# Modulation sums interleaved with the first norm, and the second row block loaded from ScalarE's queue

## The chip, the core and the metric

The kernel runs on one core of one Trainium2 chip. The metric is the device time of one launch in microseconds. The core's engines run side by side, each taking its own instructions in the order in which they were built: TensorE (PE, with its weight loads as PEld), VectorE (DVE), ScalarE (ACT), GpSimd (POOL) and SyncE (SP). SP and ACT also start transfers (DMAs): such a start is an instruction in that engine's own stream, shown in the trace as SPq or ACTq.

## The reference

One block with adaptive layer norm, in float32, on 2048 rows of 512 columns:

```python
mod = (_silu(c) @ w_mod).reshape(c.shape[0], 6, 1, -1)
sa, ca, ga, sb, cb, gb = (mod[:, 0], ..., mod[:, 5])
h = _layernorm(x, axis=-1) * (1 + ca) + sa
x = x + ga * _A_ref(h, A_dft_seq_re, A_dft_seq_im, A_dft_hid_re, A_dft_hid_im)
h = _layernorm(x, axis=-1) * (1 + cb) + sb
x = x + gb * _B_ref(h, B_w1, B_w3, B_w2)
```

`_A_ref` multiplies by a 512 x 512 transform along the columns and a 2048 x 2048 transform along the rows and keeps the real part; `_B_ref` is a gated product through 1792 hidden columns. Only the very first part matters here: the norm of the first rows, the two modulation vectors `sa` and `1 + ca` (six vectors come from one matrix of 512 x 3072; these two are needed first), and the first products along the columns.

## The kernel before

The rows are handled in eight row blocks k of 2 x 128 rows (a block of rows and its mirror image, the two "sides"). Each block is loaded, normed, turned with TensorE, modulated, added to and subtracted from its mirror image, split into a high and a low part, and multiplied with the weights of the column transform. Those weights come in four blocks (`load_hid`, tile `w`), each of four loads of 64 x 512; ScalarE copies a high part (`w_highs`, tile `wu`), VectorE takes the low part (`w_lows`) and ScalarE a negated copy (`w_minus`, tile `wn`).

The modulation vectors are sums over 512 rows of `w_mod`. `v` is 1 for `1 + ca` and 0 for `sa`; each comes as two tiles `wmr` (h = 0, 1) with two groups of 128 rows in each (n = 0, 1). ScalarE scales the first group by `silu(c)` (L335), VectorE adds the three others onto it (L307), four matmuls against ones then sum over the partitions into a bank (`mod_sum`, L314), and VectorE reads the bank into `mod` (`mod_read`, L324). Only then can ScalarE modulate the turned rows (`hm`, L501).

What comes before the modulated rows of block 0 is written out by hand in the order shown in the diff below. Everything behind that is put in order by a planner (`arrange`) with a table of ranks and estimated times of its own; its table is not touched. `keep_warm` issues matmuls whose result is not used. `clear_z` copies zeros into a tile that the first bank of products is begun with (`hid_begin`, L549). In the norm, `norm_stats` is L449 and L450, `norm_root` a square root on ScalarE (L454), `norm_inverse` L459 and L460, `norm_scale` L468 and L470, and `turn_rows` L485.

Loads are tracked by eight semaphores, taken in turn (DMAHW0 to DMAHW7 below). A load that takes a semaphore which an earlier load used is held, on the engine that starts it, until that earlier load has landed.

```python
    nc.sync.dma_start(cc, cp)
    load_x(0, nc.scalar)
    load_wm(1, 0, nc.scalar)
    load_wm(1, 1, nc.sync)
    load_wm(0, 0, nc.scalar)
    load_wm(0, 1, nc.sync)
    for dt in range(2):
        load_hid(dt, nc.sync)
    load_x(1)
```

Of the kernel before, what the change touches and what calls it, by code (L numbers as in the profile page):

```python
# [12 lines left out]
OP = mybir.AluOpType  # L13
AX = mybir.AxisListType

P = 128
# [26 lines left out]
def folded(nc, pools, c, cp, wmr, wmc, x, xt, ctr, cti, wdr, wdi, w1, w3, w2, out):  # L43
# [15 lines left out]
    def take(dt=F32, what="s"):  # L59
        slot = free.popleft()  # L60
        count[0] += 1
        t = big.tile([P, 2, N], dt, name=f"{what}_{count[0]}", tag=f"slot{slot}")
        slot_of[id(t)] = (slot, t)
        return t

    def give(t):
        slot, _ = slot_of.pop(id(t))
        free.append(slot)

    def bank(i):  # L70
        count[0] += 1
        return psum.tile([P, N], F32, name=f"bank{i}_{count[0]}", tag=f"bank{i}")

    def flat(t):
        return t.rearrange("p a b -> p (a b)")
# [7 lines left out]
    def cols(i):  # L83
        return slice(i * P, (i + 1) * P)

    def copy(dst, src, scale=1.0):
        nc.scalar.activation(dst, src, AF.Copy, scale=scale)  # L87
# [57 lines left out]
    def where(k):  # L145
        return k % (NK // 2), 1 - k // (NK // 2)
# [19 lines left out]
    def load_mirror(dst, src, k, t=None):  # L166
        i, par = where(k)
        rows = src.rearrange("i p q n -> (i p q) n" if t is None else "t i p q n -> (t i p q) n")
        at = mirror[:, t or 0, 1 - par, i : i + 1]
        nc.gpsimd.indirect_dma_start(  # L170
            dst, None, rows, bass.IndirectOffsetOnAxis(ap=at, axis=0)
        )
# [25 lines left out]
    xz = {}  # L198

    held = consts.tile([1, 1], F32, name="held")  # L200

    def load_x(k, other=nc.sync):
        if k >= NK // 2:
            nc.gpsimd.tensor_copy(held, wd[0][0:1, 1, 0:1].bitcast(F32))


        i, par = where(k)
        xz[k] = take(F32, "x")
        nc.sync.dma_start(xz[k][:, 0, :], x[i][par::2])
        if par:  # L210
            other.dma_start(xz[k][:, 1, :], x[NK - 1 - i][1::2])
        else:
            load_mirror(xz[k][:, 1, :], x, k)

    wm = {}
# [10 lines left out]
    def load_hid(dt, queue):  # L226
        i, par = HD[dt]
        raw_w[dt] = take(F32, "w")
        for m, w in enumerate((wdr, wdi)):
            for q in range(2):  # L230
                queue.dma_start(raw_w[dt][q * 64 : (q + 1) * 64, m, :], w[i][par::2, q])
# [6 lines left out]
    load_wm(0, 1, nc.sync)  # L238
    for dt in range(2):
        load_hid(dt, nc.sync)  # L240
    load_x(1)
    for dt in range(2, ND):
        load_hid(dt, nc.sync)
    for k in range(2, 4):
# [26 lines left out]
    zero = take(F32, "zero")  # L271
    nc.gpsimd.memset(flat(zero), 0.0)
    first_tmp = take(F32, "tmp")
    onesf = first_tmp[:, 0, :]
# [3 lines left out]
    def keep_warm(count, width=N):  # L278

        for _ in range(count):  # L280
            nc.tensor.matmul(
                warm[:, :width], onesf[:, :P], onesf[:, :width], start=True, stop=True
            )

    sc = consts.tile([P, ND], F32, name="sc")
# [8 lines left out]
    def hid_cols(t, dt):  # L294

        i, par = HD[dt]
        return t[:, 2 * P * i + par : 2 * P * (i + 1) : 2]

    mod_acc = [bank(5), bank(6)]

    def mod_scale(v, h):

        w, own = wm[v, 0][:, 0, :], wm[v, h]
        if h == 0:
            copy_by(w, w, sc[:, 0:1])
        for n in range(1 - h, 2):
            nc.vector.scalar_tensor_tensor(  # L307
                w, own[:, n, :], sc[:, 2 * h + n : 2 * h + n + 1], w, op0=OP.mult, op1=OP.add
            )

    def mod_sum(v):

        for dt in range(ND):
            nc.tensor.matmul(  # L314
                mod_acc[v][:, cols(dt)],
                hid_cols(wm[v, 0][:, 0, :], dt),
                onesf[:, :P],
                start=True,
                stop=True,
            )  # L320

    def mod_read(v):
        for at in (slice(0, ND),) if v else [slice(dt, dt + 1) for dt in range(ND)]:
            nc.vector.tensor_scalar(  # L324
                mod1[:, v, at],
                mod_acc[v][:, ::P][:, at],
                float(v),
                None,
                op0=OP.add,
            )  # L330
        for h in range(2):
            give(wm.pop((v, h)))

    def copy_by(dst, src, by):
        nc.scalar.activation(dst, src, AF.Identity, scale=by)  # L335
# [106 lines left out]
    def norm_stats(k, side):  # L442
        if side == 0:
            rs[k] = (
                small.tile([P, 2, 2], F32, name=f"mv_{k}", tag="mv"),
                small.tile([P, 2, 2], F32, name=f"rs_{k}", tag="rs"),
            )
        st = small.tile([P, 6], F32, name=f"st_{k}_{side}", tag="st")
        nc.vector.bn_stats(st, xz[k][:, side, :])  # L449
        nc.vector.bn_aggr(rs[k][0][:, side, :], st)  # L450

    def norm_root(k):
        mv, r = rs[k]
        nc.scalar.activation(r[:, 0, :], mv[:, :, 1], AF.Sqrt, bias=eps, scale=1.0)  # L454

    def norm_inverse(k):

        mv, r = rs[k]
        nc.vector.reciprocal(r[:, 0, :], r[:, 0, :])  # L459
        nc.vector.scalar_tensor_tensor(  # L460
            r[:, 1, :], mv[:, :, 0], -1.0, r[:, 0, :], op0=OP.mult, op1=OP.mult
        )
# [17 lines left out]
    def turn_rows(k, side):  # L480
        if side == 0:
            turned[k] = [bank(2 * (k % 2) + h) for h in range(2)]
        for dt in range(ND):
            at = (dt % 2) * HALF + side * P
            nc.tensor.transpose(  # L485
                turned[k][dt // 2][:, at : at + P],
                hid_cols(xz[k][:, side, :], dt),
                anti if side and where(k)[1] else ident,
            )
        if side:  # L490
            give(xz.pop(k))
            rs.pop(k)
# [48 lines left out]
    nought = consts.tile([P, P], F32R, name="nought")  # L541
# [4 lines left out]
    def hid_begin(k):  # L546

        hb[k] = bank(4 + k % 2)
        nc.tensor.matmul(  # L549
            hb[k], nought, flat(wt[0] if k else zz)[:, :N], start=True, stop=False, skip_group_check=True  # L550
        )
# [102 lines left out]
    def clear_z():  # L654
        copy(flat(zz), flat(zero))
        give(zero)
# [838 lines left out]
    }  # L1495
    seq_steps = []
    keep_warm(3)
    for side in range(2):
        norm_stats(0, side)
    norm_root(0)  # L1500
    norm_inverse(0)
    for side in range(2):
        norm_scale(0, side, "ACT" if side else "DVE")
        turn_rows(0, side)
    keep_warm(1)
    for v, h in ((1, 0), (1, 1), (0, 0)):
        mod_scale(v, h)
    mod_sum(1)
    copy(nought, zero[:, 0, :P])
    clear_z()  # L1510
    hid_begin(0)
    keep_warm(6, P)
    mod_scale(0, 1)
    mod_read(1)
    mod_sum(0)
    mod_read(0)


    at(10.0, "turn0.0", "turn0.1")
# [18 lines left out]
    for k in range(NK):  # L1538
        r = k * PACE
        both = [f"{k}.0", f"{k}.1"]  # L1540
        if k:
# [10 lines left out]
            for s in range(2):  # L1552
                task(
                    f"scale{k}.{s}", r + RANK["scale"] + s, [f"inverse{k}"],
                    lambda e, k=k, s=s: norm_scale(k, s, e), ACT=0.71, DVE=0.46,
# [5 lines left out]
        for dt in range(ND):  # L1561
            task(
                f"mod{k}.{dt}", r + RANK["mod"] + 0.1 * dt, [f"modc{dt}", *[f"turn{n}" for n in both]],
                lambda e, k=k, dt=dt: modulate_rows(k, dt, e), ACT=0.45, DVE=0.46,
# [1068 lines left out]
```

## Time and profile before

| | us |
|---|---|
| three runs | 691.91, 692.39, 694.4 |
| median of them | 692.39 |
| the profiled execution | 690.63 |
| its span, first to last instruction | 688.8 |
| first matmul on modulated rows (L559) begins | 21.82 |
| TensorE busy in the span | 672.4 (98%) |

The span lies 1.83 us under the profiled execution's own time, and that execution 1.76 us under the median. Times in the views are us from the span's start, and a duration follows a start. The granted TensorE clock is 0.997 over the span.

### The profile page before, as it was taken

To read this page: it belongs to the slowest core of one execution; us is meant where nothing else is said; L and a number is where in the kernel's file an instruction comes from. 1 tells how busy PE (TensorE), PEld (TensorE's weight loads), DVE (VectorE), ACT (ScalarE), POOL (GpSimd) and SP (SyncE) were. 2 spreads that over 40 slices of the span, in tenths; PEclk is the share of its full clock that TensorE was granted. 3 is DMA by queue.
4 is the path that set the end of the run, shared out by engine and by line. 5 is a ranking of instruction groups with operands and counts; after the bars stand their busy time and mean duration, and the time that the engine had idled before them with its cause. 6 is when DMAs were issued, how large, how long until landed. Compare 5 with 4: busy or idle time off the path is not lost.

```text
span 688.8 us, 9035 instructions
## 1 busy us (share of the span) xinstructions
PE 672.4 (98%) x3122; PEld 557.4 (81%) x3122; DVE 586.8 (85%) x945; ACT 451.2 (65%) x751; POOL 132.2 (19%) x156
## 2 busy tenths in 40 slices
PE   6999999999999999999999999999999999999996
PEld 4898788888888888888788888887887888888785
DVE  5999769998999987989997989787998979888465
ACT  4998956455343665663577767867687887877620
POOL 1320162543435000100101001011011112221100
PEclk9999999999999999999999999999999999999998
DMA  8740299787679440274767666475859998999713
GB/s 264 224 124 1 54 368 339 249 297 258 197 287 291 154 151 30 46 139 122 119 141 141 150 153 121 94 128 118 267 108 183 175 203 167 181 214 173 179 45 127
DMA packets 40837, 116.80 MB, mean 170 GB/s; under 512 B 5200, under 2 KB 5456, under 8 KB 40784
## 3 DMA queue, kind: packets, MB, share of 16 engines
q0 software_dynamic: 14512, 50.86, 36.9%
q1 hardware_dynamic: 25840, 63.98, 28.1%
q10 hardware_dynamic: 432, 1.31, 0.6%
q8 instruction: 26, 0.43, 0.3%
q14 instruction: 27, 0.22, 0.1%
HBM read 76.81 MB, written 41.42 MB: 172 GB/s over the span
## 4 chain that ended last, share of the span: by engine, by line
PE 84%; DVE 9%; ACT 4%; issue 1%; DMA 1%; SPq 0%; DVEq 0%; ACTq 0%
PE bank L100 54%; PE bank L750 26%; PE bank L559 2%; PE bank L598 1%; ACT hm L501 1%; DMA x<-in_x 1%; DVE xr L806 1%; DVE st L449 1%; PE bank L576 1%; DVE v L96 1%; DVE hl L90 0%; DVE ul L90 0%; DVE x L93 0%; ACT hh L87 0%; DVE w3s L90 0%
## 5 line engine op out<-in xcount | busy, mean ns | idle before, releaser
L100 PE MATMUL bank<-hf,w2h 128*128 128x512 f32 (+1 forms) x352 | 108.3, 389 | 0.0
L87 ACT ACTIVATE hf<-v 128x512 fp32r<-128x512 f32 x71 | 44.4, 631 | 66.7 <-DVE v L96 53.9
L335 ACT ACTIVATE y<-bank,gb 128x512 f32<-128x512 f32 x118 | 76.5, 682 | 3.9 <-PE bank L100 3.6
L100 PEld LDWEIGHTS bank<-hf,w2h 128*128 128x128 f32 x352 | 65.6, 188 | 15.4 <-ACT y L335 1.5
L1161 POOL DMA_DIRECT2D sum<-y x28 | 24.0, 857 | 240.7 <-ACT y L335 124.5
L100 PE MATMUL bank<-hf,w2l 128*128 128x512 f32 (+1 forms) x176 | 68.1, 387 | 0.0
L90 DVE TENSOR_TENSOR hf<-v,hf 128x512 fp32r<-128x512 f32 x71 | 48.7, 685 | 10.6 <-ACT hf L87 10.5
L1353 POOL DMA_DIRECT2D sum<-y x35 | 29.8, 852 | 128.3 <-ACT y L335 120.8
L87 ACT ACTIVATE x<-bank 128x512 f32<-128x512 f32 x72 | 41.7, 591 | 13.6 <-PE bank L100 12.7
L750 PE MATMUL bank<-d,uh 128*128 128x512 f32 x128 | 49.9, 390 | 0.0
L750 PE MATMUL bank<-l,us 128*128 128x512 f32 x128 | 49.9, 390 | 0.0
L750 PE MATMUL bank<-d,us 128*128 128x512 f32 x128 | 49.9, 390 | 0.0
L750 PE MATMUL bank<-bh,us 128*128 128x512 f32 x128 | 49.9, 390 | 0.0
L750 PE MATMUL bank<-bh,ul 128*128 128x512 f32 x128 | 49.8, 389 | 0.0
L750 PE MATMUL bank<-l,uh 128*128 128x512 f32 x128 | 49.8, 389 | 0.0
L170 POOL DMA_INDIRECT re<-in_ctr,mirror x32 | 35.7, 1115 | 66.6 <-ACT im L188 40.1
L170 POOL DMA_INDIRECT im<-in_cti,mirror x32 | 32.9, 1028 | 33.4 <-DVE l L90 8.9
L100 PEld LDWEIGHTS bank<-hf,w2l 128*128 128x128 f32 x176 | 33.1, 188 | 6.6
L93 DVE TENSOR_TENSOR v<-bank,x 128x512 f32<-128x512 f32 x36 | 24.7, 686 | 15.6 <-PE bank L100 14.0
L1245 ACT ACTIVATE v<-v 128x512 f32<-128x512 f32 x36 | 22.6, 629 | 22.7 <-DVE v L93 22.4
L93 DVE TENSOR_TENSOR x<-bank,x 128x512 f32<-128x512 f32 x36 | 24.7, 685 | 14.5 <-PE bank L100 13.7
L188 ACT ACTIVATE im<-l 128x512 f32<-128x512 f32 x16 | 10.1, 632 | 32.4 <-DVE d L93 15.5
(260 smaller groups left out, 1922.4 us busy)
## 6 DMA issues: line engine op xcount, KB each, us to landing
sum<-y POOLq DMA_DIRECT2D x63, 512.0 KB, 5.7
w<-in_w SPq DMA_DIRECT2D x42, 512.0 KB, 4.8
re<-in_ctr SPq DMA_DIRECT2D x32, 256.0 KB, 5.8
im<-in_cti SPq DMA_DIRECT2D x32, 256.0 KB, 5.3
wmc<-in_wmc SPq DMA_DIRECT2D x8, 512.0 KB, 7.2
sum<-xr SPq DMA_DIRECT2D x8, 512.0 KB, 5.6
x<-in_x SPq DMA_DIRECT2D x11, 256.0 KB, 4.5
xr<-in_xt SPq DMA_DIRECT2D x8, 256.0 KB, 7.1
```

The lines of the kernel that those rows point to most:

```text
L87: nc.scalar.activation(dst, src, AF.Copy, scale=scale)
L90: nc.vector.tensor_tensor(out=dst, in0=a, in1=b, op=OP.subtract)
L93: nc.vector.tensor_tensor(out=dst, in0=a, in1=b, op=OP.add)
L100: nc.tensor.matmul(acc, lhs[a], rhs[b], start=first and n == 0, stop=last and n == len(PASSES) - 1, skip_group_check=more,)
L170: nc.gpsimd.indirect_dma_start(dst, None, rows, bass.IndirectOffsetOnAxis(ap=at, axis=0))
L188: nc.scalar.activation(to, src.bitcast(F32), AF.Square, accum_out=chk[:, kind, KINDS.index(m), n : n + 1],)
L335: nc.scalar.activation(dst, src, AF.Identity, scale=by)
L559: nc.tensor.matmul(halves(hb[k])[:, m, :], sides((hh, hl)[a][k])[:, dt, m, :], wu[dt][:, b, m, :], start=False, stop=dt % 2 == 1 and n == ...
L750: nc.tensor.matmul(acc[what, e], lhs, rhs, start=begin and i == 0, stop=(end or (turn and what == "x")) and i == len(terms) - 1, skip_grou ...
L1161: nc.gpsimd.dma_start(sums[t, d // 2], y, accum_op=OP.add)
L1245: behind(k != 0 or q == 0, lambda: nc.scalar.activation(v, src, AF.Silu))
L1353: nc.gpsimd.dma_start(sums[t, which], y, accum_op=OP.add)
```

## The change

The zeros are copied right at the start. The first scaling and the first addition for `v = 1` stand ahead of and behind the square root of the norm. The first matmul that was only there to keep TensorE busy becomes one that writes zeros over the whole bank for `v = 0`; that vector's sum over the partitions is then made in two parts, one for tile h = 1 (whose first group ScalarE scales, where VectorE added it before) and one for tile h = 0 with the rest added onto it. The load of row block 1 leaves SP's queue, where it stood between the second and the third block of column weights, and is issued from ScalarE's instruction stream behind its modulation copies.

```diff
-    def load_x(k, other=nc.sync):
+    def load_x(k, other=nc.sync, one=nc.sync):
...
-        nc.sync.dma_start(xz[k][:, 0, :], x[i][par::2])
+        one.dma_start(xz[k][:, 0, :], x[i][par::2])
...
-    load_x(1)
     for dt in range(2, ND):
         load_hid(dt, nc.sync)
...
-    def mod_scale(v, h):
-
+    def mod_copy(v, h, n):
+        w = wm[v, h][:, n, :]
+        copy_by(w, w, sc[:, 2 * h + n : 2 * h + n + 1])
+
+    def mod_add(v, h, n):
         w, own = wm[v, 0][:, 0, :], wm[v, h]
-        if h == 0:
-            copy_by(w, w, sc[:, 0:1])
-        for n in range(1 - h, 2):
-            nc.vector.scalar_tensor_tensor(
-                w, own[:, n, :], sc[:, 2 * h + n : 2 * h + n + 1], w, op0=OP.mult, op1=OP.add
-            )
-
-    def mod_sum(v):
+        nc.vector.scalar_tensor_tensor(
+            w, own[:, n, :], sc[:, 2 * h + n : 2 * h + n + 1], w, op0=OP.mult, op1=OP.add
+        )
+
+    def mod_begin():
+        nc.tensor.matmul(
+            mod_acc[0], zero[:, 0, :P], onesf, start=True, stop=False, skip_group_check=True
+        )
+
+    def mod_sum(v, h=0, apart=False):
 
         for dt in range(ND):
             nc.tensor.matmul(
                 mod_acc[v][:, cols(dt)],
-                hid_cols(wm[v, 0][:, 0, :], dt),
+                hid_cols(wm[v, h][:, 0, :], dt),
                 onesf[:, :P],
-                start=True,
-                stop=True,
+                start=not apart,
+                stop=not apart or h == 0,
+                skip_group_check=apart,
             )
...
     keep_warm(3)
+    copy(nought, zero[:, 0, :P])
+    clear_z()
     for side in range(2):
         norm_stats(0, side)
+    mod_copy(1, 0, 0)
     norm_root(0)
+    mod_add(1, 0, 1)
     norm_inverse(0)
     for side in range(2):
         norm_scale(0, side, "ACT" if side else "DVE")
         turn_rows(0, side)
-    keep_warm(1)
-    for v, h in ((1, 0), (1, 1), (0, 0)):
-        mod_scale(v, h)
+    mod_begin()
+    mod_add(1, 1, 0)
+    mod_copy(0, 0, 0)
+    mod_add(1, 1, 1)
+    mod_copy(0, 1, 0)
+    load_x(1, nc.scalar, nc.scalar)
     mod_sum(1)
-    copy(nought, zero[:, 0, :P])
-    clear_z()
+    mod_add(0, 0, 1)
+    mod_sum(0, 1, True)
+    mod_add(0, 1, 1)
+    keep_warm(1, P)
+    mod_sum(0, 0, True)
+    mod_read(1)
+    mod_read(0)
     hid_begin(0)
-    keep_warm(6, P)
-    mod_scale(0, 1)
-    mod_read(1)
-    mod_sum(0)
-    mod_read(0)
```

On ScalarE, from its second table load to the modulated rows of block 0, the order before was this (`mv` and `rs` belong to the norm of block 0, `x_87` is row block 0, `w_99` and `w_104` the first two blocks of column weights; the brackets name what an instruction waits for):

```order
L286 ACTIVATE sc<-cc 128x4 [waits DMAHW1_49]
L454 ACT_TABLE_LOAD
L454 ACTIVATE rs_162<-mv_161,eps 128x2 [waits DVE_49]
L468 ACTIVATE x_87<-x_87,rs_162 128x512 [waits DMAHW0_49,DVE_49]
L335 ACTIVATE wmr_90<-wmr_90,sc 128x512 [waits DMAHW3_49,Activation_49]
L335 ACTIVATE wmr_94<-wmr_94,sc 128x512 [waits DMAHW5_49]
L87 ACTIVATE nought<-zero_140 128x128 [waits Pool_49]
L87 ACTIVATE z_156<-zero_140 128x1024
L87 ACTIVATE wu_216<-w_99 128x256 [waits DMAHW1_49,DMAHW0_49]
L87 ACTIVATE wu_216<-w_99 128x256 [waits DMAHW3_49,DMAHW2_49]
L501 ACTIVATE hm_219<-bank_19_173,mod_147 128x256 [waits DVE_49] x2
```

and of the change it is this (`x_190` is row block 1):

```order
L285 ACTIVATE sc<-cc 128x4 [waits DMAHW1_49]
L87 ACTIVATE nought<-zero_137 128x128 [waits Pool_49]
L87 ACTIVATE z_153<-zero_137 128x1024
L340 ACTIVATE wmr_90<-wmr_90,sc 128x512 [waits DMAHW3_49,Activation_49]
L459 ACT_TABLE_LOAD
L459 ACTIVATE rs_161<-mv_160,eps 128x2 [waits DVE_49]
L473 ACTIVATE x_87<-x_87,rs_161 128x512 [waits DMAHW0_49,DVE_49]
L340 ACTIVATE wmr_94<-wmr_94,sc 128x512 [waits DMAHW5_49]
L340 ACTIVATE wmr_96<-wmr_96,sc 128x512 [waits DMAHW6_49]
L209 DMA x_190<-in_x 128x1x512 [waits DMAHW6_49]
L211 DMA x_190<-in_x 128x1x512 [waits DMAHW0_49]
L87 ACTIVATE wu_215<-w_99 128x256 [waits DMAHW1_49]
```

The table load that the square root needs now stands behind the first scaled copy, which waits for a load (DMAHW3), and both copies of the first column weights and the modulated rows stand behind two load starts that wait for DMAHW6 and DMAHW0.

On SP, at the place where row block 1 was loaded, the starts before were these (`x_109` is row block 1 there, `w_112` the third block of column weights):

```order
L231 DMA w_104<-in_wdr 64x512 [waits DMAHW4_49]
L231 DMA w_104<-in_wdr 64x512 [waits DMAHW5_49]
L231 DMA w_104<-in_wdi 64x512 [waits DMAHW6_49]
L231 DMA w_104<-in_wdi 64x512 [waits DMAHW7_49]
L209 DMA x_109<-in_x 128x1x512 [waits DMAHW0_49]
L211 DMA x_109<-in_x 128x1x512 [waits DMAHW1_49]
L231 DMA w_112<-in_wdr 64x512 [waits DMAHW2_49]
```

and of the change these (`w_109` is the third block of column weights, `w_114` the fourth):

```order
L231 DMA w_104<-in_wdi 64x512 [waits DMAHW6_49]
L231 DMA w_104<-in_wdi 64x512 [waits DMAHW7_49]
L231 DMA w_109<-in_wdr 64x512 [waits DMAHW0_49]
L231 DMA w_109<-in_wdr 64x512 [waits DMAHW1_49]
L231 DMA w_109<-in_wdi 64x512 [waits DMAHW2_49]
L231 DMA w_109<-in_wdi 64x512 [waits DMAHW3_49]
L231 DMA w_114<-in_wdr 64x512 [waits DMAHW4_49]
L231 DMA w_114<-in_wdr 64x512 [waits DMAHW5_49]
L231 DMA w_114<-in_wdi 64x512 [waits DMAHW7_49]
```

The third block of column weights took the place of row block 1. DMAHW6 was last used by the third load into `w_104`, and DMAHW0 by the first load into `w_109`, when ScalarE's two load starts ask for them.

## The prediction

> **What bounds the kernel now.** First the page, for what the end hangs on; then the chain of waits over the first 60 us, since the change touches nothing behind that.
>
> ```profile
> span 688.8 us, 9035 instructions
> PE 84%; DVE 9%; ACT 4%; issue 1%; DMA 1%; SPq 0%; DVEq 0%; ACTq 0%
> ```
>
> ```profile
> 1.19 4.54 DMA x<-in_x
> ...
> 7.50 0.30 ACT rs L454
> ...
> 8.94 0.72 ACT wmr L335
> ...
> 14.84 0.95 PE bank L314 x8
> ...
> 15.82 0.17 DVE mod L324
> 15.99 0.02 issue
> 16.02 0.09 ACT hm L501
> ...
> 28.54 0.53 ACT h L87
> 29.07 0.04 issue
> 29.12 1.21 PE bank L598 x4
> ```
>
> The chain runs from row block 0's load through the norm's root, the modulation sums (TensorE at 14.84, read at 15.82) to the first modulated rows (`hm`, 16.02). From there to 29.1 it stays on ScalarE almost without a gap, and behind that it is TensorE, VectorE and ScalarE in turn, with DMA at 1% of the whole. So a microsecond won or lost at `hm` goes to the end: nothing behind it waits for a transfer that could take it up. What counts is when ScalarE can begin `hm`, then whether row block 1 comes in time.
>
> **ScalarE's own rows** (timeline) show where the change cuts in:
>
> ```profile
> 3.90 0.20 ACT L286 ACTIVATE sc<-cc 128x4 f32<-128x4 f32 x1
> 4.12 1.28 ACT L454 ACT_TABLE_LOAD   x1
> 7.50 0.30 ACT L454 ACTIVATE rs<-mv,eps 128x2 f32<-128x2 f32 x1 [2.09 <-DVE mv L450]
> 8.22 0.81 ACT L468 ACTIVATE x<-x,rs 128x512 f32<-128x512 f32 x1 [0.43 <-DVE rs L460]
> 10.90 1.04 ACT L87 ACTIVATE z<-zero 128x1024 fp32r<-128x1024 f32 x1
> 13.66 0.42 ACT L87 ACTIVATE wu<-w 128x256 fp32r<-128x256 f32 x1 [0.54 <-DMA w<-in_wdi]
> 16.93 0.72 ACT L87 ACTIVATE wu<-w 128x256 fp32r<-128x256 f32 x2
> 17.54 1.05 ACT L87 ACTIVATE wn<-wu 128x1024 fp32r<-128x1024 f32 x1
> ```
>
> The table load lies at 4.12, well before the root at 7.50. ScalarE is idle for most of 13.7 to 16.0: `wu` of the first column weights, its last work there, is done by 14.1.
>
> **Zeros first: nothing won.** The copies (0.29 and 1.04 us) move from 10.70 to 4.1, into the idle time before 7.5. Their old place ended at 11.94, before ScalarE waited for column weights anyway.
>
> **The table load comes late: 1.73 us, hidden.** In the change the first scaled copy stands ahead of the square root's table load, and waits for its `wmr` load. That one's landing, and the landings used below, are single answers of the DMA view (us from issue to landing at the end):
>
> ```profile
> wmr<-in_wmr ACTq DMA_DIRECT2D x1, 512.0 KB, 5.8
> w<-in_wdi SPq DMA_DIRECT2D x1, 128.0 KB, 4.7
> x<-in_x SPq DMA_DIRECT2D x1, 256.0 KB, 4.1
> w<-in_wdi SPq DMA_DIRECT2D x1, 128.0 KB, 3.9
> 1.41 1.16 ACTq L220 DMA_DIRECT2D wmr<-in_wmr  x2
> 10.60 1.52 SPq L231 DMA_DIRECT2D w<-in_wdi  x2
> 12.18 0.59 SPq L209 DMA_DIRECT2D x<-in_x  x1
> 12.81 0.60 SPq L211 DMA_DIRECT2D x<-in_x  x1
> ```
>
> Issued at 1.41, it lands at 7.21. The copy takes 0.72, so the table load begins at 7.93 and, at 1.28, the root can begin at 9.23 instead of 7.50: the norm and the turn move back by 1.73. VectorE's first addition (0.75) fits into that wait.
>
> The skill weighs in here: the Trainium skill, "ScalarE: Activation LUTs", section "What ACT_TABLE_LOAD costs", puts a switch at 1283 ns for the load and some 1380 ns more for a drain. The load agrees with 1.28; of the drain the trace shows nothing, as the load at 4.12 follows directly on an instruction that ended at 4.10. By the page the root would move another 1.38 and the modulation vectors would be read at 17.2, not 15.8, still within the hold on ScalarE that is worked out below, so the sum stays.
>
> On TensorE the rows are
>
> ```profile
> 2.60 4.51 PE L281 MATMUL bank<-tmp 128*128 128x512 f32 x6 [2.60 <-DVE tmp L275]
> 8.92 0.72 PE L485 MATMUL bank<-ident,x 128*128 128x128 f32 x4 [1.81 <-DVE x L470]
> 9.95 1.02 PE L281 MATMUL bank<-tmp 128*128 128x512 f32 x2
> 13.34 1.50 PE L281 MATMUL bank<-tmp 128*128 128x128 f32 x12
> ```
>
> The matmul behind the turn begins at 9.95 + 1.73 = 11.68. `mod_begin` has the shape of that keep-warm matmul: 1.02, to 12.70. The sums for `v = 1`, ready by then on VectorE (two additions of 0.75 behind the scale, 12.0), take 0.95 as in the chain: 13.65. The part sum of tile h = 1 takes 0.95 more: 14.60; its ScalarE copy is done at 12.1. The narrow keep-warm is two of the passes of 1.50 / 12: 0.24, to 14.84. Then comes the last part, 0.95, for which VectorE's adds are done at 13.5. That is the time at which the last sums began before (14.84), so the vectors are read at 15.8 as before. The late table load has eaten what the earlier start of the sums gave: 0.0 here.
>
> **Row block 1 on ScalarE's stream: +1.5.** This is the term that decides. Behind its three copies (done at 12.1) ScalarE has to start two loads. By the order of the change the first is held until the third load into `w_104` has landed, which is the last user of its semaphore: issued at 10.60, 4.7 us on the way, 15.3. That such holds are real, SP's own waits show:
>
> ```profile
> SPq L231 <- DMA wmr<-in_wmr: 3.2, 4, 1.6
> ```
>
> A start takes 0.60 (the row at 12.81), so it is away at 15.9. The second is held by the first load into `w_109`, which has taken row block 1's place on SP, at 12.18. No row shows it there; the load that was issued at 12.18 took 4.1, so I take 16.28, and with a start of 0.60 ScalarE is free at 16.88. Queued behind are `wu` of the first column weights (two copies, 0.61 from 16.93 to 17.54) and then `hm`, for which TensorE, VectorE and all of block 0 wait: `hm` begins at 17.5 instead of 16.02, **+1.5**.
>
> Next, row block 1 itself. VectorE's rows:
>
> ```profile
> 18.92 0.66 DVE L449 BATCH_NORM_STATS2 st<-x 128x6 f32<-128x512 f32 x1
> 19.62 0.18 DVE L450 BATCH_NORM_AGGREGATE mv<-st 128x2 f32<-128x6 f32 x1
> 19.72 0.66 DVE L93 TENSOR_TENSOR hs<-hm 128x512 f32<-128x512 f32 x1
> 21.13 0.63 ACT L87 ACTIVATE hh<-hs 128x512 fp32r<-128x512 f32 x1
> ```
>
> Its second half, issued at 16.28, lands at 20.4 by the same 4.1, against 16.9 before. The second `st` then ends at 21.1 and `mv` at 21.3, and `hs` behind them on VectorE begins at 21.3: +1.6, while `hm` is ready at 21.0. Its reader `hh` on ScalarE comes at 21.13 + 1.5 = 22.6, when the first half of `hs` has been done since 22.0. So lateness of row block 1 costs next to nothing on top; if its halves took 0.7 us longer, it would take over.
>
> On SP the third and fourth block of column weights start 1.28 us sooner (12.18 for 13.46). That wins nothing where `hm` is late: their copies stand behind it.
>
> **The sum and its bounds.** +0.0 from the sums, +1.5 from the hold: 690.63 + 1.5 = 692.1 for a profiled execution (span 690.3), and 692.39 + 1.5 = **693.9** as a median, as the shown execution lay 1.76 under the median. For the load that holds the second start, the neighbouring rows go from 3.9 to 4.7. Below, even a load of 3.1 would leave the first start in the way: free at 16.5, +1.1. Above, 16.88 and a start of 0.63: +2.1. That it wins is excluded as long as the first start waits for 15.3. So the forecast's own range is 693.5 to 694.5.
>
> **Rivals.**
>
> *The starts do not hold ScalarE (692.2, not slower).* The place is the two load starts on ScalarE. If the semaphores they ask for are free when ScalarE gets there, because they stand for older loads (a `wmr` half, in by 10.6, and the first load into `w_99`, which SP saw landed at 12.18), they go out at 12.1 and 12.8, ScalarE does `wu` at 13.4 and `hm` begins at 16.0 as before. Row block 1 lands as before, and 0.1 to 0.2 us come off a later wait for the fourth block of weights. The point is the first start: gone by 14.8 the hold is nothing. Against it: in the order of the change, the copy of the fourth load of `w_104` no longer waits for the third, as if ScalarE had already waited for it.
>
> *Faster (690.8).* If, besides, the table load ran while the copy waits for its weights, the turn would stay at 8.92 to 10.1, VectorE's additions would end at 12.5, and TensorE, from 10.1 with 1.02 + 3 x 0.95 + 0.24, would read out at 14.3: `hm` at 14.4, -1.6. The order puts that load behind the copy on one stream, which speaks against it.
>
> *TensorE goes cold (694.1 to 696.3).* It idles from 7.11 to 8.92 now, and to 10.65 in the change: 3.5 us. Its first passes were slow:
>
> ```profile
> 4.47 0.34 PEld L281 LDWEIGHTS bank<-tmp 128*128 128x128 f32 x1 [0.52 <-issue]
> 5.32 0.34 PEld L281 LDWEIGHTS bank<-tmp 128*128 128x128 f32 x1 [0.52 <-issue]
> ```
>
> 0.85 apart, against 0.51 for a pass at 9.95. If 3.5 us ran so again (as from 2.60 to about 6.1), 1.4 us would be lost and the vectors read at 17.2; `hm` would wait for them until 17.5 to 17.7, +1.5 to +1.7. If all sums ran cold, 5.2 us would become 8.7, and the whole is +3.9 or so. Idle for 1.8 us cost nothing at 8.92. The Trainium skill, "TensorE: Matmul & The Clock Gate", in its Part 1, has the clock halved after an idle window of some 3.4 us; this idle would lie just at that figure, and no row here shows an idle so long.
>
> **How the numbers follow.** Forecast 0.62, starts that do not hold 0.18, cold TensorE 0.13, faster 0.07. The range is **691.7 to 695.6**: it takes in the not-slower rival and most of the cold one, with about 1 us for the scatter of the runs shown (691.91 to 694.4), and leaves out the faster one. A measurement of this kernel tells some 0.5%, or 3.5 us, from no change: faster than that 0.02, slower 0.07 (the far cold end and scatter), within 0.91.
>
> **What would show it.** In the profile of the change: the second table load at about 7.9 and the root at 9.2; two starts on ScalarE's queue at about 15.3 and 16.3, idle before; `hm` near 17.5; vectors read near 15.8; `L598` at 29.12 about 1.5 later; the rest the same. `hm` before 16.5 makes the forecast wrong, and so does a root near 7.5 or a gap that opens behind 30 us.

## The result, and the profile after

The changed kernel took 694.55 us (median of ten runs, 692.78 to 695.67) beside 692.15 us for the kernel before on the same chip (ten runs, 690.8 to 694.4): a ratio of 1.0032, 95% interval 1.0018 to 1.0046, which is 1.2 to 3.2 us slower. (The ratios here are those of the means, and can differ a little from what two medians give.) The forecast was +1.5 us and 693.9. The profiled execution took 693.49 us; it lies 1.06 under its median, and the one before lay 1.52 under this median. The two profiles can be set side by side to about half a microsecond: they differ by 2.9, the medians by 2.4.

The page gives the span and the shares of the chain of waits:

```profile
span 691.7 us, 9024 instructions
PE 83%; DVE 9%; DMA 3%; ACT 2%; SPq 1%; issue 1%; DVEq 0%; ACTq 0%
```

DMA went from 1% to 3% of the chain and ScalarE from 4% to 2%: where the start-up was a chain of ScalarE work, it now runs through landings. TensorE's timeline tells how much of the loss lies in the start-up. The first product of the row transform is a good mark for its end; here it is of the kernel before, and then of the change:

```profile
83.72 0.39 PE L750 MATMUL bank<-bh,us 128*128 128x512 f32 x1
```

```profile
86.64 0.39 PE L755 MATMUL bank<-bh,us 128*128 128x512 f32 x1
```

It comes 2.92 later, and the spans differ by 2.9. So everything was lost ahead of it. The experiments are read at this mark too, with two limits. The profile before is a quick execution of its kernel, so a mark set against it shows up to 1.5 us too much. And some profiles lose more behind the mark, 0.7 to 1.2 us in four of them; with the starts alone, for one, TensorE waited 0.89 for VectorE at 134 us.

**ScalarE's rows** of the change (start, duration, what; in brackets the idle time before and what ended it):

```profile
7.33 0.72 ACT L340 ACTIVATE wmr<-wmr,sc 128x512 f32<-128x512 f32 x1 [2.06 <-DMA wmr<-in_wmr]
8.07 1.28 ACT L459 ACT_TABLE_LOAD   x1
9.36 0.30 ACT L459 ACTIVATE rs<-mv,eps 128x2 f32<-128x2 f32 x1
...
10.81 1.32 ACT L340 ACTIVATE wmr<-wmr,sc 128x512 f32<-128x512 f32 x2
15.34 0.54 ACTq L209 DMA_DIRECT2D x<-in_x  x1
16.32 0.55 ACTq L211 DMA_DIRECT2D x<-in_x  x1
16.92 0.72 ACT L87 ACTIVATE wu<-w 128x256 fp32r<-128x256 f32 x2 [4.79 <-DMA w<-in_wdr]
17.72 1.02 ACT L506 ACTIVATE hm<-bank,mod 128x256 f32<-128x256 f32 x2
...
22.97 0.29 ACT L459 ACTIVATE rs<-mv,eps 128x2 f32<-128x2 f32 x1 [0.82 <-DVE mv L455]
```

The two load starts stand at 15.34 and 16.32 (forecast: 15.3 and 16.28), and behind 12.1 ScalarE does nothing until 16.92. The 4.79 us are put down to a `w` load, but the kernel before had that tile at 12.71:

```profile
12.71 0.42 ACT L87 ACTIVATE wu<-w 128x256 fp32r<-128x256 f32 x1 [0.76 <-DMA w<-in_wdr]
```

The first experiment below, with all of the change but the two starts, has it at 12.64. So the starts were what held. A start does not count as busy time, so its hold shows up as idle time of the next computation, under another name. `hm` begins at 17.72 instead of 16.02. The root of block 1, at 20.34 before, comes at 22.97: 1.70 late at `hm`, 2.63 late there. VectorE's rows say why, and the answer on the DMAs started between 15 and 16.9 us gives the landing (`hs` is a block plus its mirror image, `hh` the high part of that, which the first products need):

```profile
17.52 0.35 DVE L329 TENSOR_SCALAR mod<-bank 128x1 f32<-128x1 f32 x4 [1.94 <-PE bank L318]
...
22.03 0.69 DVE L454 BATCH_NORM_STATS2 st<-x 128x6 f32<-128x512 f32 x1 [1.32 <-DMA x<-in_x]
...
22.86 0.66 DVE L93 TENSOR_TENSOR hs<-hm 128x512 f32<-128x512 f32 x1
```

```profile
x<-in_x ACTq DMA_DIRECT2D x2, 256.0 KB, 5.7
```

Row block 1's second half, started at 16.32, was 5.7 us on the way and not 4.1. The statistics wait 1.32 for it, and `hs` stands behind them on VectorE at 22.86 although `hm` is done by 21.2.

The sums were not read at 15.8 either, but at 17.52. TensorE's rows, and the windows (busy us of each engine with its count, then the granted clock, the DMA engines' share, GB/s):

```profile
10.78 0.72 PE L490 MATMUL bank<-ident,x 128*128 128x128 f32 x4 [2.69 <-DVE x L475]
11.33 1.01 PE L490 MATMUL bank<-anti,x 128*128 128x128 f32 x4
12.13 1.91 PE L311 MATMUL bank<-tmp,zero 128*128 128x512 f32 x2
13.84 2.48 PE L318 MATMUL bank<-tmp,wmr 128*128 128x128 f32 x16
...
24.45 0.50 PE L564 MATMUL bank<-wu,hh 128*128 128x256 f32 x2 [1.16 <-ACT hh L87]
```

```profile
11.00:11.50 0.50, 0.50 (x6) 0.50 (x6) 0.47 (x2) 0.50 (x2) 0.00 (x0) 0.90 1.03 217
11.50:14.50 3.00, 3.00 (x10) 1.96 (x10) 2.00 (x3) 0.63 (x2) 0.00 (x0) 0.50 1.03 255
14.50:15.00 0.50, 0.50 (x5) 0.50 (x5) 0.00 (x0) 0.00 (x0) 0.00 (x0) 0.69 1.05 283
```

After an idle time of 2.69 us TensorE's granted clock was 0.50 for 3.4 us, and `mod_begin` took 1.91 where 1.02 was reckoned. Yet `hm` at 17.72 is only 0.2 later than forecast: without late sums it could have begun at about 17.5, behind the two `wu` copies. Two delays lay side by side there, and one of them had not been in the forecast.

### The profile page after: what moved, and what is told of

Its sections match the earlier page's. It is cut to its first block, busy times and chain, and to the rows that moved or that the text cites. A ratio compares the mean times of both kernels' runs of the same rounds, so it can differ in the third digit from the quotient of the medians.

```text
span 691.7 us, 9024 instructions
## 1 busy us (share of the span) xinstructions
PE 674.6 (98%) x3120; PEld 558.5 (81%) x3120; DVE 586.2 (85%) x944; ACT 452.5 (65%) x752; POOL 135.2 (20%) x156
## 4 chain that ended last, share of the span: by engine, by line
PE 83%; DVE 9%; DMA 3%; ACT 2%; SPq 1%; issue 1%; DVEq 0%; ACTq 0%
PE bank L100 54%; PE bank L755 25%; PE bank L564 2%; DMA wmr<-in_wmr 1%; PE bank L603 1%; DMA x<-in_x 1%; DMA w<-in_wdr 1%; DVE hl L90 1%; DVE xr L811 1%; PE bank L581 1%; DVE v L96 1%; SPq L231 0%; DVE ul L90 0%; DVE x L93 0%; DVE st L454 0%
## 5 line engine op out<-in xcount | busy, mean ns | idle before, releaser
L90 DVE TENSOR_TENSOR hf<-v,hf 128x512 fp32r<-128x512 f32 x71 | 48.7, 686 | 10.4 <-ACT hf L87 10.3
L170 POOL DMA_INDIRECT im<-in_cti,mirror x32 | 35.0, 1095 | 30.8 <-PE bank L755 10.1
L93 DVE TENSOR_TENSOR v<-bank,x 128x512 f32<-128x512 f32 x36 | 24.7, 686 | 15.9 <-PE bank L100 14.9
L1250 ACT ACTIVATE v<-v 128x512 f32<-128x512 f32 x36 | 22.6, 629 | 22.8 <-DVE v L93 22.5
```

The costliest lines, as they stand in the source:

```text
L90: nc.vector.tensor_tensor(out=dst, in0=a, in1=b, op=OP.subtract)
L93: nc.vector.tensor_tensor(out=dst, in0=a, in1=b, op=OP.add)
L170: nc.gpsimd.indirect_dma_start(dst, None, rows, bass.IndirectOffsetOnAxis(ap=at, axis=0))
L1250: behind(k != 0 or q == 0, lambda: nc.scalar.activation(v, src, AF.Silu))
```

## The experiments

The theory: the two load starts on ScalarE hold everything queued behind them, and they bring row block 1 late; the rest of the change wins nothing and costs little. The rivals: the sums themselves are late (the table load, TensorE's clock), and would have cost as much without the starts. Each kernel was timed beside the kernel before on the same chip; all of them compute the whole result.

### Row block 1 back on SP's queue, the rest of the change as it is

```diff
+    load_x(1)          # between the second and third block of weights
...
-    load_x(1, nc.scalar, nc.scalar)
```

> The changed kernel with row block 1 loaded on SP again, at its old place between the second and the third block of column weights; all else as changed. Theory A (the two load starts on ScalarE, by holding it and by bringing row block 1 in late, make the loss of 2.4 us; the late sums lie behind them): row block 1 in by 17.5 instead of 22.0, the norm's root of block 1 at about 21.9 instead of 22.97, because the sums are still read at about 17.5; 1.1 to 1.5 us off the changed kernel, so 693.2 to 693.5. Theory B (the late table load and the half clock of TensorE make all of it, and the starts cost nothing): same as the changed kernel, 694.5.

Measured: 692.78 beside 691.57 us, ratio 1.0019 (1.0009 to 1.0028). The mark came at 85.31, 1.59 later than before. ScalarE, and TensorE up to the mark:

```profile
17.62 1.02 ACT L507 ACTIVATE hm<-bank,mod 128x256 f32<-128x256 f32 x2 [3.55 <-DVE mod L330]
```

```profile
10.69 1.10 PE L491 MATMUL bank<-ident,x 128*128 128x128 f32 x4 [2.88 <-DVE x L476]
...
12.44 1.91 PE L312 MATMUL bank<-tmp,zero 128*128 128x512 f32 x2
...
85.31 0.39 PE L756 MATMUL bank<-bh,us 128*128 128x512 f32 x1
```

Half of the loss stayed, though nothing holds ScalarE now: `hm` waits 3.55 for the sums. TensorE idled 2.88 and ran at half clock from 10.8 to 14.2. So the late sums are a second cause, which the starts merely covered. This run also gives the price of a late `hm`, whatever makes it late: `hm` is 1.60 late, the root of block 1 1.61 (21.95) and the mark 1.59, with row block 1 in time.

### The table load ahead of the first copy

A square root of one constant per row, whose result nobody reads, brings the table in at 4.12:

```diff
+    early = consts.tile([P, 1], F32, name="early")
+    nc.scalar.activation(early, eps, AF.Sqrt)
```

> The changed kernel with a square root of one column put ahead of the copies of zeros, so that its table is loaded at 4 us; all else as changed. The two load starts on ScalarE take other semaphores in this build (those of the second and fourth load into the second block of column weights), so the hold ends near 16.0 to 16.7 rather than 16.9. Theory A: the norm's root returns to about 8.0, TensorE stays at full clock, the sums are read at about 15, but the modulated rows still begin at 16.7 to 17.4 and row block 1 lands at 21 or later: at most 0.8 us off the changed kernel, 693.7 to 694.5. Theory B: 2.4 us or more off it, 692.1 or less.

Measured: 694.47 beside 691.57, ratio 1.0039 (1.0024 to 1.0055): no better than the change. The root came at 8.11, but `hm` only at 17.44, as the starts still stood at 15.14 and 16.16. The sums were ready at about 16.3 and waited for ScalarE. That is the other half of the argument: with the starts in place, `hm` does not follow earlier sums. The time of the whole shows it less clearly, as TensorE's clock was halved twice in this execution, from 9.3 to 12.7 and again from 26.4 to 29.8, the second time behind an idle time of 2.76 ahead of `hh`. Row block 1's second half was seen by VectorE at 22.43 and the root of block 1 at 23.38, later still than in the change.

### The kernel before with nothing but row block 1 on ScalarE's stream

```diff
-    load_x(1)          # on SP
...
     clear_z()
+    load_x(1, nc.scalar, nc.scalar)
```

> The kernel before with one part of the change alone: row block 1 loaded from ScalarE's stream, behind the copies of zeros; sums, table load and matmuls as before. Theory A: ScalarE held until about 16.9 and row block 1 in at 22.0 as in the changed kernel, root of block 1 at about 22.9; most of the loss, 694.0 to 694.6 against 692.2. Theory B: 692.2, no loss.

Measured: 694.84 beside 691.57, ratio 1.0042 (1.0029 to 1.0054). This one move makes a loss as large as the change's, and more than the 1.8 to 2.4 us that were expected, with sums that are read as early as before (15.70) and TensorE at full clock up to there. `hm` came at 17.14, +1.12, since the starts went out 0.4 earlier than in the change. Behind it TensorE and the windows show a new cost:

```profile
23.80 0.80 PE L558 MATMUL bank<-wu,hh 128*128 128x256 f32 x2 [2.56 <-ACT hh L87]
```

```profile
24.00:26.00 2.00, 2.00 (x10) 1.93 (x11) 2.00 (x6) 2.00 (x5) 0.00 (x0) 0.50 1.04 382
```

The 50 narrow matmuls that keep TensorE busy end at 21.2; waiting for `hh` it idles 2.56, and its clock halves at 23.6. In the change they end later with the sums, the wait is 1.16, and the clock holds: late sums moved the idle time to the front. Another 1.2 us were lost behind the mark.

### More matmuls to keep TensorE busy at the start

```diff
-    keep_warm(3)
+    keep_warm(5)
```

> The changed kernel with two more keep-warm matmuls at the start (five instead of three), so that TensorE is idle for under 2 us ahead of the first turn; all else as changed. Both theories: granted clock 1.00 from 11 to 15 us instead of 0.50, sums read at about 15.9 instead of 17.5. Theory A: the modulated rows begin at 17.5 instead of 17.7 and row block 1 is late all the same, so within 0.3 us of the changed kernel, 694.3. Theory B: 1.5 us off it, 693.0.

Measured: 695.84 beside 691.57, ratio 1.0057 (1.0042 to 1.0073): no gain on the change, and some 1.7 us more loss, which neither side had expected. The clock stayed at 1.00 from 7 to 25, as meant, and the sums were ready at about 16.6. But `hm` came at 18.26, since in this execution the starts went out at 15.67 and 17.02, and TensorE, out of filler at 22.4, then idled 2.89 before `hh` and lost its clock at 25.6. So `hm` did not come sooner with the clock mended: it waited for the starts. What the half clock costs the change as a whole is not settled, for row block 0 landed 1.1 us later here than in the change, and the clock fell all the same, later.

### The hold by itself

To part the hold from the lateness, the kernel before got row block 2 on ScalarE's stream, which is not needed before 24 us; row block 1 stays on SP.

```diff
-    for k in range(2, 4):
-        load_x(k)
+    load_x(3)
...
     clear_z()
+    load_x(2, nc.scalar, nc.scalar)
```

> The kernel before with row block 2, which is not needed before 24 us, loaded from ScalarE's stream behind the copies of zeros, and row block 1 left on SP. ScalarE is held at the same place and by loads that land at the same times (15.3 and 16.3), but row block 1 is not late. If the hold has a price of its own, modulated rows begin at 17.2 to 17.5 instead of 16.0 and the kernel ends 1.0 to 1.5 us later than before. If only the lateness of row block 1 costs, it is the kernel before, within 0.4 us.

Measured: 693.22 beside 691.83, ratio 1.0019 (1.0007 to 1.0031), about +1.3 us. ScalarE:

```profile
15.04 0.54 ACTq L209 DMA_DIRECT2D x<-in_x  x1
16.07 0.54 ACTq L211 DMA_DIRECT2D x<-in_x  x1
16.66 0.72 ACT L87 ACTIVATE wu<-w 128x256 fp32r<-128x256 f32 x2 [4.67 <-DMA x<-in_x]
17.29 1.00 ACT L500 ACTIVATE hm<-bank,mod 128x256 f32<-128x256 f32 x2
...
24.33 0.42 ACT L87 ACTIVATE wu<-w 128x256 fp32r<-128x256 f32 x1 [0.60 <-DMA w<-in_wdr]
...
25.33 0.42 ACT L87 ACTIVATE wu<-w 128x256 fp32r<-128x256 f32 x1 [0.58 <-DMA w<-in_wdi]
25.65 0.61 ACT L87 ACTIVATE hh<-hs 128x512 fp32r<-128x512 f32 x1
```

and the last of these in the kernel before:

```profile
22.98 0.63 ACT L87 ACTIVATE hh<-hs 128x512 fp32r<-128x512 f32 x1
```

`hm` is 1.27 late and so is block 1's root (21.59 for 20.34). The separation is not clean: row block 2 now travels beside the fourth block of weights, whose two copies wait 0.60 at 24.33 and 0.58 at 25.33. The `hh` behind them is 2.67 late, and the mark 2.74. So in this profile only 1.3 of the 2.7 us come from the hold; the 1.3 us of the whole cannot be given to the hold alone.

### The lateness by itself

Here nothing holds ScalarE. The kernel before loads row block 1 on SP, but behind the fourth block of weights:

```diff
-    load_x(1)
     for dt in range(2, ND):
         load_hid(dt, nc.sync)
+    load_x(1)
```

> The kernel before with row block 1 moved behind the fourth block of column weights on SP: late, but no engine held, sums and table load as before. If lateness alone makes the loss: block 1's second half in at 21.5 to 22.3, its root at 22.4 to 23.2 against 20.3, TensorE idle behind its keep-warm matmuls, 2.0 us or more above the kernel before, as with the starts on ScalarE (3.3 above it there). If the hold on ScalarE makes it: within 0.7 us of the kernel before.

Measured: 695.57 beside 691.74, ratio 1.0058 (1.0042 to 1.0074), some 4 us. `hm` began at 16.06 as ever. VectorE, TensorE and the windows:

```profile
21.41 0.69 DVE L449 BATCH_NORM_STATS2 st<-x 128x6 f32<-128x512 f32 x1 [3.18 <-DMA x<-in_x]
...
23.25 0.69 DVE L449 BATCH_NORM_STATS2 st<-x 128x6 f32<-128x512 f32 x1 [0.93 <-DMA x<-in_x]
```

```profile
25.68 0.79 PE L559 MATMUL bank<-wu,hh 128*128 128x256 f32 x2 [4.26 <-ACT hh L87]
```

```profile
27.00:29.00 2.00, 2.00 (x11) 2.00 (x10) 2.00 (x5) 2.00 (x6) 0.00 (x0) 0.50 0.64 246
```

The second half lands 1.2 later than in the change, the root of block 1 comes at 24.20 (+3.86), and TensorE idles 4.26 and runs at half clock behind it. So lateness of row block 1 has a price of its own, with nothing held and no sum late.

### Row block 1 on SP and the early table load together

> The changed kernel with both: row block 1 on SP at its old place, and the square root's table loaded at 4 us. VectorE's first addition still stands ahead of the norm's reciprocal. If late starts and late sums are the whole loss: block 1 in time, sums read at 16.0 to 16.3 as in the run with the early table, modulated rows at 16.3 against 16.0 before, so within 0.4 us of the kernel before. If something else of the change costs too (the additional matmul that writes zeros, the third copy on ScalarE), it stays 1 us or more above the kernel before.

Measured: 691.69 beside 691.74, ratio 0.9998 (0.9984 to 1.0011). With the starts and the late table load taken away the loss is gone, as expected. In the profiled execution the sums were still read at 16.76: row block 0 landed 0.9 us later than before (its statistics began at 6.68), TensorE idled 1.96, and its clock halved once more, from 11.5 to 14.9. The mark came at 84.64.

### The first addition moved behind the norm

In the kernel before this one, VectorE's first addition stands ahead of the reciprocal that the norm needs. It goes behind the scaling:

```diff
-    mod_add(1, 0, 1)   # ahead of norm_inverse
...
+    mod_add(1, 0, 1)   # behind the turn
```

> As the last one, with VectorE's first addition moved behind the norm's scale, so that the norm and the turn are where they were before (turn at about 8.9). Theory: the sums are read at 14.2 to 14.6 and the modulated rows begin there, 1.5 us sooner than before; ScalarE then meets the third and fourth block of column weights, which land at 19.0 and 22.4 behind row block 1 on SP, and waits for them: 0.3 to 0.6 us off the kernel before. Rival (the weights' landing binds nothing): 1.3 us or more off it.

Measured: 692.13 beside 691.74, ratio 1.0000 (0.9989 to 1.0011). Neither the expected gain nor its rival's: row block 0 landed late again (7.36), TensorE idled 2.70 and lost its clock, and `hm` came at 17.45, not at 14.2 to 14.6. By itself it decides nothing.

### Row block 1 on GpSimd's queue

A start that waits may wait on an engine that has nothing else to do. On top of the kernel above, GpSimd begins the load when the `wmr` tile of v = 0, h = 0 has landed:

```diff
+    nc.gpsimd.tensor_copy(held, wm[0, 0][0:1, 1, 0:1])
+    load_x(1, nc.gpsimd, nc.gpsimd)
```

> As the last one, with row block 1 loaded from GpSimd's queue, which has nothing else to do there, begun when the first tile of the second modulation vector has landed (10.0). No computing engine is held, and the column weights start on SP 1.28 us sooner. Theory: modulated rows at 14.2 to 14.6, block 1 in by 17, fourth block of weights in by 21.2; 1.0 to 1.6 us off the kernel before. Rival (the loads share the same 16 DMA engines, so the weights land no sooner): as the last one.

Measured: 692.52 beside 691.74, ratio 1.0005 (0.9993 to 1.0016): none of the 1.0 to 1.6 us that were expected. Row block 1 is no longer late (root of block 1 without a wait for it), and nothing holds ScalarE. But row block 0 landed at 7.59 in this execution, TensorE idled 3.34, and the clock was halved for twice as long:

```profile
10.00:10.50 0.50, 0.00 (x0) 0.00 (x0) 0.46 (x2) 0.44 (x1) 0.06 (x1) 0.52 1.04 393
10.50:16.50 6.00, 5.75 (x21) 4.74 (x22) 3.85 (x7) 2.43 (x5) 1.48 (x3) 0.50 1.06 270
16.50:17.00 0.50, 0.50 (x5) 0.50 (x4) 0.00 (x0) 0.00 (x0) 0.00 (x0) 0.66 1.06 258
```

### One more matmul ahead: all causes gone

Row block 1 on SP, early table, addition behind the norm, and `keep_warm(4)` for 3:

> The run with row block 1 on SP, the early table and the addition behind the norm, with a fourth keep-warm matmul ahead of the first turn, so that TensorE is idle for less than 2 us there. If the half clock is what took the gain of the earlier sums in that run, the clock stays at 1.00, the sums are read at 14.4 to 15.2 and the kernel is 0.3 to 1.0 us faster than before. If not, same as that run and as before, 691.7 to 692.1.

Measured: 691.54 beside 691.83, ratio 0.9993 (0.9982 to 1.0004). Here the earlier sums stand by themselves, with the causes of the loss removed: the clock is at 1.00 over the start-up, TensorE idles 0.17 before the turn, and `hm` comes a full 1.05 sooner than before.

```profile
14.97 1.02 ACT L507 ACTIVATE hm<-bank,mod 128x256 f32<-128x256 f32 x2 [0.95 <-DVE mod L330]
...
21.32 0.42 ACT L87 ACTIVATE wu<-w 128x256 fp32r<-128x256 f32 x1
22.55 0.42 ACT L87 ACTIVATE wu<-w 128x256 fp32r<-128x256 f32 x1 [0.81 <-DMA w<-in_wdi]
22.87 0.61 ACT L87 ACTIVATE hh<-hs 128x512 fp32r<-128x512 f32 x1
```

And it wins next to nothing: the interval takes in no gain at all, and the mark is at 83.63 for 83.72. The 1.05 us are given back at 22.55, where ScalarE waits for the fourth block of weights; the `hh` behind it begins at 22.87, against 22.98 before. (Up to there all was about 1.05 ahead: the first `hh` at 20.09 for 21.13.)

### The same with row block 1 on GpSimd's queue

> The same fourth keep-warm matmul in the run with row block 1 on GpSimd's queue. With the clock at 1.00 and the column weights sooner, sums read at 14.4 to 15.2 and 1.0 to 1.6 us off the kernel before; if the weights land no sooner, as the run on SP; if the wait of GpSimd for the second vector's tile holds the turn, as one trace suggested (TensorE waited for it ahead of the first turn), no gain.

Measured: 692.27 beside 691.83, ratio 1.0006 (0.9991 to 1.0021): no gain. With row block 1 begun at 10.4, the second block of weights is late (`wu` waits 0.90 for it until 18.46), row block 0 landed at 7.39, and `hm` came at 16.24. The trace puts TensorE's idle time of 2.84 ahead of the turn down to GpSimd's wait, but the turn began 1.41 behind the root, as in the run on SP (1.40): the wait did not hold it.

### The fourth block of weights sooner

If that block took up the gain, bring it in earlier: on GpSimd's queue, on top of the kernel with all causes gone.

```diff
-    for dt in range(2, ND):
-        load_hid(dt, nc.sync)
+    load_hid(2, nc.sync)
...
+    nc.gpsimd.tensor_copy(held, raw_w[0][0:1, 1, 0:1])
+    load_hid(3, nc.gpsimd)
```

> The run before with the early table, four keep-warm matmuls and row block 1 on SP read the sums 1.04 us sooner, and yet the first products on the marker of the start-up (the first L750 matmul) came at 83.63 against 83.72, as ScalarE then waited for the fourth block of column weights (wu at 22.55). Here only that block moves from SP's queue to GpSimd's, begun once the third load into the first block of weights has landed. Theory (the fourth block took up the gain): its copies come before 22, hh near 22.0 instead of 22.9, the marker at 82.8 to 83.2, and the median 0.4 to 0.9 us under the kernel before (ratio 0.9987 to 0.9994). Rival (the transfers share the DMA engines): row block 1 or the second and third block of weights land later by as much, hh stays at 22.8 or later, the marker at 83.6 or above, and the time is equal to that of the run before or up to 1 us longer.

Measured: 696.24 beside 692.18, ratio 1.0067 (1.0047 to 1.0086). The theory's gain did not come; the rival had the direction, but allowed for 1 us at most. Two parts of the loss have to be kept apart. At the mark (86.24) the profile is 2.5 us behind the kernel before, and its last computation ends 2.6 behind (685.21 for 682.61). But the span is 4.9 us longer. The other 2.3 lie behind all computation: from there to the end of the span it is 8.5 us here, and 5.9 to 6.4 in every other profile. What they are is not shown; they are no loss of the start-up. The starts on SP and on GpSimd (the fourth block beside the third), and ScalarE:

```profile
13.64 1.24 SPq L231 DMA_DIRECT2D w<-in_wdr  x2
14.93 1.23 SPq L231 DMA_DIRECT2D w<-in_wdi  x2
```

```profile
13.70 1.27 POOL L231 DMA_DIRECT2D w<-in_wdr  x2
14.96 1.04 POOL L231 DMA_DIRECT2D w<-in_wdi  x2
```

```profile
22.31 0.42 ACT L87 ACTIVATE wu<-w 128x256 fp32r<-128x256 f32 x1 [1.52 <-DMA w<-in_wdi]
```

The fourth block was there without a wait, but the third, which is needed first, landed at 22.3 (in the kernel with all causes gone its copies were done without a wait, from 19.48). The fourth block was not its only new neighbour: with four starts fewer on SP, row block 2 began at 16.21, for 18.46 in the kernel with all causes gone. Then `hh` was late, TensorE idled 1.85, and its clock was 0.64 and 0.50 in the 4 us behind 23. The DMA engines were busy throughout, at a share of 1.02 to 1.08 from 9 to 23 us. In the kernel before they were so up to 17. Its windows (granted clock, DMA share and GB/s at the end):

```profile
9.00:11.00 2.00, 1.98 (x10) 1.15 (x10) 1.28 (x2) 1.58 (x5) 0.00 (x0) 1.00 1.06 339
11.00:13.00 2.00, 0.94 (x8) 0.94 (x8) 1.93 (x4) 1.24 (x2) 0.00 (x0) 1.00 1.08 278
13.00:15.00 2.00, 2.00 (x19) 1.96 (x18) 1.29 (x3) 0.54 (x2) 0.00 (x0) 1.00 1.04 264
15.00:17.00 2.00, 2.00 (x20) 2.00 (x20) 1.18 (x7) 0.98 (x3) 0.00 (x0) 1.00 1.01 295
```

Their share is 1.01 to 1.08 from 9 to 17 us, and then 0.93, 0.82 and 0.73 in windows of 2 us. While it is at 1.0, one load moved up should push another back; this run, the one before it (the second block late) and the hold by itself (the fourth block late) are the cases seen. A start on another engine's queue gave no way around that. The Trainium skill ("DMA: Bandwidth & Descriptors", "Issuing engines are not separate DMA queues") says that a load started from another engine uses the same 16 DMA engines, and the run agrees with its 22.3.

## Why the prediction was right, and where its sizes were off

**The forecast's mechanism was right**: the two starts on ScalarE hold `wu` and `hm`. They stood at 15.34 and 16.32 for 15.3 and 16.28. That the second came so near was luck in part: the load that it waited for started at 12.45, not 12.18, and took 3.9, not 4.1. The 1.5 of the sum is borne out by the rows (`hm` 1.70 late) and by the run with late sums alone, where an `hm` 1.60 late puts the mark 1.59 back, at 1.0019, about 1.3 us. The run meant to give the hold by itself measures 1.0019 too, but mixes in late weights. The rival by which the starts find their semaphores free is refuted by the two rows of the starts.

**Zeros first: nothing won.** Right; the copies ran at 4.03 and 4.23.

**The table load late by 1.73.** The size was right: the root came at 9.36, 1.86 late, as the copy began at 7.33 and not at 7.21. The drain of the Trainium skill ("ScalarE: Activation LUTs", "What ACT_TABLE_LOAD costs") did not appear: the root follows the 1.28 us of the load within 0.01.

**The sums read at 15.8.** Wrong: 17.52. The step that failed was to count TensorE's passes at the durations of the profile before. The rival with the cold TensorE, at 0.13, had this part right (it said 17.2). Its far end, +3.9, does not follow from its own figures: 8.7 us of sums for 5.2 is 3.5 more. It did not set the time, because the hold reaches to the same place, 17.5. That was chance: with row block 1 back on SP, these sums cost 1.0019 by themselves. To speak of "0.0 here" as though the term were harmless was wrong; it was hidden, and the hold was its cover.

**Row block 1 late: "next to nothing on top".** This is the term that was mis-sized. The landing was taken as 4.1 us, from a load which stood ahead of the third and fourth block of weights. (The second half itself took 4.3 in the profile before; 4.1 was the first.) Behind the starts of those weights (SP had issued the third block and begun on the fourth by 16.32) the same load took 5.7. That its new neighbours made it slower is argued from the DMA share of 1.0, not shown by a run of its own. The prediction had the bound: "if its halves took 0.7 us longer, it would take over". They took 1.6 longer, and the root of block 1 was 2.63 late with `hm` 1.70 late: 0.9 more. The remaining 0.3 up to the mark's 2.92 arises behind it. The prediction's own sign, `L598` at 29.12 some 1.5 later, came 2.91 later (L603, 32.03). That lateness has such a price was shown by the run with row block 1 late on SP, without any hold: 1.0058.

**What bounds the kernel.** "Nothing behind it waits for a transfer that could take it up" holds for a loss at `hm`, not for a gain. With `hm` 1.05 sooner and nothing else worse, the time was 0.9993 (0.9982 to 1.0004), as the fourth block of weights landed at 22.4 to 22.5. The faster rival's condition was thus brought about, in large part, and its 1.6 us did not follow; SP begins that block at the same time in both (17.3 before, 17.2 there, its second half). Before, its last load started at 17.9 and took 4.6, so it was in at 22.5, and its copy began at 22.67: the slack was 0.2 us.

**The parts add up otherwise than a sum.** Row block 1's move alone costs 1.0042, the late sums alone 1.0019, both together 1.0032. A delay ahead of `hm` is shared by all that wait there, and late sums push TensorE's filler matmuls back, over the wait for `hh`. The intervals of 1.0042 and 1.0032 overlap, so their order is not shown.

## What to carry to other kernels

A load start is an instruction in its engine's stream: if it may have to wait for a semaphore, put it where nothing urgent stands behind it, and read its hold as idle time of the next computation, whatever releaser that row names. How long a load takes can depend on what was started ahead of it (4.1 and 5.7 us here); while the DMA share is at 1.0, price a moved load by its new neighbours, and expect one moved up to push another back. Before making one thing ready sooner, look for the next input that lands: the slack that it shows in the old profile (0.2 us here) bounds what can be won, as long as that input lands no sooner.

## What was not expected of the hardware

**TensorE's clock falls for stretches of one length, after idle times that differ.** In the change the half clock lasted from 11.40 to 14.81 (from the shares of the half microseconds around: 0.90 and 0.69), 3.4 us; with row block 1 on GpSimd's queue from 10.02 to 16.84, 6.8 us, twice that. Worked out the same way, the other profiles in which the clock fell give 3.4 us each time, and 6.8 in the one with row block 1 late on SP. The Trainium skill ("TensorE: Matmul & The Clock Gate", Part 1) has a free-running window of 3413 ns, and these two lengths agree. Its rule of thumb against idle times above some 3 us ("Why this matters for your kernels") was too lenient here: the clock fell within 1.5 us of the end of idle times of 1.96, 2.56, 2.69 and 2.88 us, and of 1.85 in the last run. It did not fall near one of 1.81 (before), nor near 1.94 (ahead of the turn in the last run), nor near 2.84 (row block 1 on GpSimd's queue with one more matmul). Where the idle time lies against the window could explain this; no run here moved one against the other, and whether the transposes between idle time and the next full matmul count as work stays open too.

**The first load varies.** VectorE could begin on row block 0 at 5.76 in the profile before, at 6.41 in the change, and between 5.63 and 7.59 in the experiments, though these first starts were never touched. It need not be chance alone: the four profiles of kernels made from the one before lie at 5.63 to 5.80, the ten of kernels made from the change at 5.89 to 7.59, in this order on each of the three chips that ran both in the experiments. Why is not shown, and no run tried it. A late landing lengthens TensorE's first idle time (1.81 us before, 2.70 with a landing at 7.36), and can so bring the clock down; single profiles of the start-up, those above among them, differ by this as well, so where a profile and the medians disagree, the medians count.
